# DeltaNet and SwiGLU on one core: chunk 1's second half of feed-forward units by block products, the first keys loaded in halves, 32x32 first scores, split last stores

## The chip, the core and the metric

The kernel runs on one core of a Trainium2 chip. The core has five engines that run side by side, each with its own queue in order: TensorE (PE; its weight loads are shown apart as PEld), VectorE (DVE), ScalarE (ACT), GpSimd (POOL) and SyncE (SP, which here only issues DMAs). Matmul results land in one of eight PSUM banks and have to be copied out by DVE or ACT. The metric is the device time of one execution in microseconds (us).

## The reference

Four batches, eight heads, 768 positions, head size 48. The first part is a recurrence over the positions of each head, with normalised keys; its output, 3072 tokens of 384 numbers, goes through an RMS norm and a SwiGLU feed-forward (FFN) with 1536 hidden units.

```python
k_n = k / (np.linalg.norm(k, axis=-1, keepdims=True) + 1e-06)
for t in range(S):
    y[:, :, t] = np.einsum('bhd,bhde->bhe', q[:, :, t], state)
    v_old = np.einsum('bhde,bhd->bhe', state, kt)
    state = state + bt[:, :, :, None] * np.einsum('bhd,bhe->bhde', kt, vt - v_old)
x = y, with the heads side by side                       # 3072 x 384
xn = x / np.sqrt(np.mean(x * x, axis=-1, keepdims=True) + 1e-06) * rms_g
g, val = xn @ w_gate, xn @ w_val                         # 3072 x 1536 each
out = (g * (1 / (1 + np.exp(-g))) * val) @ w_out         # 3072 x 384
```

All arithmetic is in 32-bit floats. The three weight matrices of the FFN come as 64-bit floats and are converted on the core.

## The kernel before

**Chunks.** The sequence is cut into 12 chunks of 64 positions; a chunk holds 256 tokens of the FFN. For each chunk, `prep` multiplies its keys with each other (`scores`, L690) and inverts the triangular matrix that follows from them in 15 steps of two VectorE instructions (L987, L993), `recur` applies the running state and brings the normalised tokens into the tile `xf` (chunk 1: `xp1`), and the FFN turns them into output rows. Chunk 0 has its own path, `prep_first`: it transposes the keys (`turn`), takes 64x64 scores, copies the 32x32 blocks on their diagonal into `sq1` (L775, L777), turns them into `sq2` and `at16`, multiplies those by an outer product of key norms and betas (L797, L800), and inverts 16x16 blocks in 7 steps. The key norms come from `norms`: a square on ScalarE (L711), a sum on VectorE (L712), a power on GpSimd (L715).

**The FFN has two forms.** `ffn_plain` multiplies directly: for each of 12 slices f of 128 hidden units, six matmuls of 128x128 by 128x256 (L1430, gate and value), a SiLU and a product, then two matmuls of 128x128 by 128x384 (L1412). A half is six slices; its partial output waits in `part` (`finish`). `ffn` and `down` use schemes with fewer block products: each half h of the hidden units takes 15 products of four 128x128 by 128x128 matmuls (L1523), whose results ScalarE copies and VectorE adds up in `tmp` (L1536, L1534), and the output projection takes 7 products of six 128x128 by 128x192 matmuls (L1581). For that the tokens are first combined (L1382), sums and differences of weight blocks are made by `factors(h)` (L1488; nine go to the tile `extra`, in `more`, and the last four, `over=True`, change `w_in` in place, after the last plain reader of that half) and by `out_factors` (L1560; the last changes `wo_sb` in place). Every product of half h waits for the last in-place factor (key `wx`). Before the change, chunks 0 and 1 go the plain way and chunks 2 to 11 the other. Each matmul on 32-bit floats is two instructions on PE.

**Weights.** `weights` brings them in 18 pieces through three buffers (`raw`, in `more`), each converted by two ScalarE instructions (L617, L618) and two VectorE instructions (L619, L620). The buffer `cva` lies in the part of `xf` that holds the combined tokens.

**Order.** All instructions are written into a plan with estimated durations, due times and a list of data that they read and write. `Plan.run` simulates the engines, orders each queue by due time and slack, tries random variations (those in `MOVES` are applied, each drawn from its own number) and emits the program in that order. `DUE0` and the like are due times, `FETCH`/`AHEAD` model how PE's instructions are fetched, and `EARLYM`/`MARGIN` are what is allowed beyond a DMA's estimated landing. Until `WARM`, gaps on PE are filled with matmuls on the identity matrix (`filler`, L1701) that compute nothing. So any change of an edit, a due time or `MOVES` rearranges all queues. The main sequence around the change is:

```python
if c == 1:
    stage(ffn_plain, 0, 0, FT // 2, due(0, 0))
    stage(ffn_plain, 1, 0, FT // 2, due(1, 0))
    stage(ffn_plain, 0, FT // 2, FT, due(1, 0) + 23)
    stage(ffn_plain, 1, FT // 2, FT, due(1, 0) + 46)
    stage(factors, 0)
    stage(factors, 1)
    stage(out_factors)
elif c > 1:
    stage(ffn, c, due(c, 0))
```

Of the kernel before, what the change touches and what calls it, by code (L numbers as in the profile page):

```python
# [14 lines left out]
ALU = mybir.AluOpType  # L15
# [9 lines left out]
ROUNDS, SEED = 24, 5  # L25
MOVES = (
# [7 lines left out]
)  # L34
FETCH, AHEAD = 67.0, 160.0
EARLY = 130.0
FETCH0, AHEAD0 = 42.0, 130.0
STICK = 2.0
SHAKE = 0.06
PATIENT = 0.3  # L40
RING, LANES, FIRST, LAND = 2330, 8, 1.08, 0.9
WARM = 60.0
CLEAR = (0.3, 0.6, 0.9)
TURNK = range(4, 12)
BEGIN = 1.7
ONSET = {"PE": 1.0, "ACT": 2.6, "DVE": 0.85, "POOL": 0.35, "SP": 0.5}
# [12 lines left out]
RUSH = 25.0  # L59
RUSHW = 0.0  # L60
# [38 lines left out]
class Plan:  # L99
# [197 lines left out]
    def vary(self, n, keys, past, clear, starts):  # L297
# [3 lines left out]
        a = rng.choice((rng.uniform(0.0, 650.0), rng.uniform(0.0, 220.0)))  # L301
# [77 lines left out]
def kernel(  # L379
# [248 lines left out]
    def load(c, what):  # L628
# [8 lines left out]
        for key, t, src, pr in (("k2", k2[c % NK], k, pk), ("q2", q2, q, pq)):  # L637
            for g in range(2):
                if key[0] not in what or key == "q2" and c > 1:
                    continue  # L640
                dst = t[64 * g : 64 * g + 64, :, 0:D]
                s = src.rearrange("b (y g) t e -> g t (b y) e", g=2)[g, t0 : t0 + C]
                dma(dst, s, pr, w=[(key, c % NK, g)] if key == "k2" else q2k[8 * g : 8 * g + 8], dur=0.7, work=1.5 if c < 3 else 1.15, desc=1024, eng="ACT" if c == 0 and g and key == "k2" else "SP", bulk=c > 0 or key == "q2")
# [8 lines left out]
    def turn(src, dst, keys, r, pr, split):  # L652

        for hv in range(2):
# [10 lines left out]
            P.add("PE", 0.55, tr, pr, r=r + ["ident"], w=[ps, keys[hv]], ps=ps, size=8)  # L665
# [37 lines left out]
    def kkeys_(c):  # L703
        return [("k2", c % NK, 0), ("k2", c % NK, 1)]

    def norms(c):
# [4 lines left out]
        P.add("ACT", A(768), lambda: nc.scalar.square(r_, kd), pn, r=kkeys_(c), w=[("r", 0), ("r", 1)])  # L711
        P.add("DVE", V(768), lambda: nc.vector.tensor_reduce(out=ksum[i2], in_=r_, axis=AXL.X, op=ALU.add), pn, r=[("r", 0), ("r", 1)], w=[("ksum", i2)], lat=0.05)  # L712

        P.add("DVE", 0.17, lambda: nc.vector.tensor_scalar_max(ksum[i2], ksum[i2], 1e-30), pn, w=[("ksum", i2)])  # L714
# [50 lines left out]
    def prep_first():  # L765
        kn, ktk, kkeys = k2[0], ktkeys(0), kkeys_(0)
        turn(kn, kt[0], ktk, kkeys + [("k2p", 0)], 0.0, True)
        ps = scores(kt[0], kt[0], 0.0, ktk, [])
        for q_ in range(4):
            rows, cols = slice(W * q_, W * q_ + W), slice(W * (q_ % 2), W * (q_ % 2) + W)  # L770
            for d in range(2):
                dst = sq1[rows].rearrange("p (x n) -> p x n", n=W)[:, d:16:2]
                src = lambda d=d, rows=rows, cols=cols, ps=ps: heads(ps[d])[rows, :, cols]
                if d:
                    P.add("DVE", 0.45, lambda dst=dst, f=src: nc.vector.tensor_copy(out=dst, in_=f()), 0.0, r=[ps[d]], w=[("sq1", q_, d)], last=ps[d])  # L775
                else:
                    P.add("ACT", A(256), lambda dst=dst, f=src: nc.scalar.copy(dst, f()), 0.0, r=[ps[d]], w=[("sq1", q_, d)], last=ps[d])  # L777
        sqk = [("sq1", q_, d) for q_ in range(4) for d in range(2)]
# [114 lines left out]
    def prep(c):  # L893
# [14 lines left out]
        fast = c < 4  # L908
# [199 lines left out]
    def recur(c):  # L1108
# [201 lines left out]
        for h in halves:  # L1310
# [42 lines left out]
            for p in h:  # L1353
# [7 lines left out]
                for k_ in range(KT):  # L1361
                    if c < 2 and p:
                        P.add("DVE", V(128), lambda p=p, psx=psx, k_=k_: nc.vector.tensor_scalar(
                            out=xdst[:, 2 * k_ + p], in0=psx.t[:, 128 * k_ : 128 * k_ + 128], scalar1=g_sb[:, k_ : k_ + 1], scalar2=None, op0=ALU.mult
                        ), pxv, r=[psx, "g"], w=[xkeys[p]], last=psx)
                        continue
# [3 lines left out]
        if c > 1:  # L1370
            X = lambda a, n, step=1: xf[:, a : a + step * (n - 1) + 1 : step]
            for dst, a, b_, op, n in (
                (X(6, 2), X(0, 2, 2), 4, ALU.add, 2),
                (X(8, 1), X(6, 1), 2, ALU.add, 1),
                (X(9, 2), X(1, 2, 2), 8, ALU.subtract, 2),
                (X(11, 2), X(1, 2, 2), 4, ALU.add, 2),
                (X(13, 2), X(1, 2, 2), 5, ALU.add, 2),
# [41 lines left out]
    def ffn_plain(c, f0, f1, start):  # L1419
# [317 lines left out]
```

## Time and profile before

| | |
|---|---|
| Time, median of 3 runs | 679.27 us (673.34 to 679.56) |
| The profiled execution: its own time | 678.64 us |
| its span, first to last instruction | 676.3 us |
| granted TensorE clock, mean | 0.997 |
| busy: PE / PEld / DVE / ACT / POOL | 97% / 90% / 79% / 46% / 18% |
| L1523, products of the hidden units, 2400 matmul instructions | 304.0 us busy |
| L1581, products of the output projection, 840 | 151.1 us busy |
| L1430 and L1412, plain FFN of chunks 0 and 1, 288 and 96 | 101.4 us busy |

The busy time of matmuls that follow each other closely overlaps: one L1523 instruction shows 277 ns, yet the next starts about 112 ns after it. The cost of matmul work is therefore read from the chain of work or the timeline, where a run of n instructions has a start and an end. PE's 97% also holds the filler of the first 57 us. "Idle before" is an engine's idle time ahead of an instruction, with what ended it.

### The profile page before, as it was taken

What the parts mean: (1) busy time and instruction counts of PE and PEld (TensorE: products, weight loads), DVE (VectorE), ACT (ScalarE), POOL (GpSimd) and SP (SyncE); (2) the same over time, 40 slices, a digit from 0 to 9 for tenths busy, and PEclk for the clock granted to TensorE, in tenths of its full rate; (3) what the DMA queues carried; (4) which work ended last, traced back from release to release, by engine and by line L of the source; (5) the groups of instructions that cost most, each with busy time, mean ns of one, the idle gap of its engine ahead of it and who ended that gap; (6) DMA issues with size and microseconds to landing.
All of it is one profiled execution on the core that took longest, in us unless ns stands there. A gap on an engine that the chain in (4) does not pass through costs nothing.

```text
span 676.3 us, 23308 instructions
## 1 busy us (share of the span) xinstructions
PE 658.9 (97%) x9896; PEld 608.1 (90%) x9896; DVE 535.4 (79%) x1142; ACT 314.3 (46%) x763; POOL 118.8 (18%) x95
## 2 busy tenths in 40 slices
PE   8889989999998999999999999999999999999997
PEld 5778767878798999999999999999999999999997
DVE  7988795999798598699699599599689649966472
ACT  5557572753255246346346345445353444344341
POOL 8400020020600320330330330330311012000000
PEclk9999999999999999999999999999999999999999
DMA  8984897956676246547446467525725532130101
GB/s 95 155 257 80 191 205 143 270 90 128 92 121 125 43 75 121 104 66 135 82 74 116 84 103 119 97 44 106 122 46 91 102 75 48 25 57 2 25 1 23
DMA packets 285976, 66.61 MB, mean 98 GB/s; under 512 B 269104, under 2 KB 276784, under 8 KB 285872
## 3 DMA queue, kind: packets, MB, share of 16 engines
q1 hardware_dynamic: 284832, 64.93, 53.0%
q8 instruction: 77, 1.26, 0.8%
q10 hardware_dynamic: 1040, 0.20, 0.2%
q14 instruction: 27, 0.22, 0.1%
HBM read 46.61 MB, written 18.48 MB: 96 GB/s over the span
## 4 chain that ended last, share of the span: by engine, by line
PE 79%; DVE 8%; DMA 6%; SPq 4%; issue 1%; ACT 1%; POOL 0%; DVEq 0%
PE bank L1523 37%; PE bank L1581 21%; PE bank L1430 5%; SPq L509 4%; PE bank L690 3%; PE bank L1412 2%; DVE acc L993 2%; DMA at<-dkk 2%; PE bank L1206 2%; DVE acc L987 2%; DMA q<-in_q_dram 2%; PE bank L1092 1%; PE bank L1143 1%; PE bank L1192 1%; PE bank L1131 1%
## 5 line engine op out<-in xcount | busy, mean ns | idle before, releaser
L1523 PE MATMUL bank<-xf,w_in 128*128 128x128 f32 x1440 | 179.8, 277 | 0.0
L1523 PEld LDWEIGHTS bank<-xf,w_in 128*128 128x128 f32 x1440 | 170.0, 192 | 1.6 <-issue 0.8
L1534 DVE TENSOR_TENSOR tmp<-tmp,bank 128x512 f32<-128x512 f32 x180 | 120.7, 681 | 43.6 <-PE bank L1523 37.7
L1523 PE MATMUL bank<-xf,more 128*128 128x128 f32 x960 | 124.2, 277 | 0.0
L1523 PEld LDWEIGHTS bank<-xf,more 128*128 128x128 f32 x960 | 115.1, 192 | 1.3
L1536 ACT COPY tmp<-bank 128x512 f32<-128x512 f32 x120 | 69.6, 585 | 81.9 <-PE bank L1523 67.3
L1540 ACT ACTIVATE tmp<-tmp 128x256 f32<-128x256 f32 x120 | 49.7, 417 | 82.7 <-DVE tmp L1534 82.4
L993 DVE TENSOR_REDUCE acc<-acc 128x30 f32<-128x90 f32 (+4 forms) x165 | 78.0, 473 | 5.7
L1581 PE MATMUL bank<-wo_sb,hf 128*128 128x192 f32 x360 | 65.6, 333 | 0.6 <-DVE hf L1541 0.6
L938 POOL TENSOR_TENSOR at<-at,bs 128x1024 f32<-128x1024 f32 x8 | 18.9, 2360 | 246.9 <-DMA at<-dkk 148.1
L1581 PEld LDWEIGHTS bank<-wo_sb,hf 128*128 128x128 f32 x360 | 59.1, 193 | 2.1 <-DVE hf L1541 0.9
L987 DVE TENSOR_TENSOR acc<-acc,at 128x60 f32<-128x60 f32 (+4 forms) x165 | 56.4, 342 | 2.6
L1541 DVE TENSOR_TENSOR hf<-tmp 128x256 f32<-128x256 f32 x120 | 49.6, 429 | 10.4 <-ACT tmp L1540 9.2
L715 POOL TENSOR_TENSOR knrm<-ksum,half 128x16 f32<-128x16 f32 x12 | 35.7, 2971 | 88.3 <-DVE ksum L714 45.4
L1430 PE MATMUL bank<-xf,w_in 128*128 128x256 f32 x144 | 34.4, 385 | 0.3 <-DVE w_in L620 0.3
L1412 PE MATMUL bank<-wo_sb,hf 128*128 128x384 f32 x96 | 33.9, 493 | 0.0
L1430 PE MATMUL bank<-xp,w_in 128*128 128x256 f32 x144 | 33.1, 382 | 0.0
L1327 POOL TENSOR_TENSOR rs<-ms,mhalf 128x2 f32<-128x2 f32 (+1 forms) x13 | 9.7, 748 | 126.0 <-DVE ms L1322 85.6
L1430 PEld LDWEIGHTS bank<-xf,w_in 128*128 128x128 f32 x144 | 26.6, 190 | 5.6 <-DVE w_in L620 0.9
L1430 PEld LDWEIGHTS bank<-xp,w_in 128*128 128x128 f32 x144 | 27.0, 190 | 4.7 <-issue 0.2
L1590 DVE TENSOR_TENSOR tmp<-tmp,bank 128x192 f32<-128x192 f32 x30 | 10.5, 350 | 25.7 <-PE bank L1581 25.6
L1412 PEld LDWEIGHTS bank<-wo_sb,hf 128*128 128x128 f32 x96 | 17.8, 190 | 10.4 <-DVE hf L1438 0.6
(185 smaller groups left out, 1000.8 us busy)
## 6 DMA issues: line engine op xcount, KB each, us to landing
at<-dkk SPq DMA_DIRECT2D x22, 256.0 KB, 4.2
vt<-in_v_dram SPq DMA_DIRECT2D x24, 192.0 KB, 4.2
more<-in_moe_w_gate_dram SPq DMA_DIRECT2D x6, 768.0 KB, 8.8
more<-in_moe_w_val_dram SPq DMA_DIRECT2D x6, 768.0 KB, 7.3
more<-in_moe_w_out_dram SPq DMA_DIRECT2D x6, 768.0 KB, 7.3
out_dram<-tmp SPq DMA_DIRECT2D x48, 96.0 KB, 2.2
k<-in_k_dram SPq DMA_DIRECT2D x23, 192.0 KB, 4.8
xd<-yn SPq DMA_DIRECT2D x36, 96.0 KB, 2.9
```

The lines of the kernel that those rows point to most:

```text
L509: op = P.add(eng, dur, lambda: queue.dma_start(out=dst, in_=src), prio, r, w, lat=0.1)
L715: P.add("POOL", 2.95 if c < 2 else 3.3, lambda: nc.gpsimd.tensor_tensor(out=knrm[i2], in0=ksum[i2], in1=half, op=ALU.pow), pn, r=[("ksum", ...
L987: nc.vector.tensor_tensor(out=acc[:, 1:3, 0:n, j + 2 : W].rearrange("p a i t -> p i a t"), in0=acc[:, old, 0:n, j : j + 2, None].to_broadc ...
L993: nc.vector.tensor_reduce(out=acc[:, new, 0:n, j + 2 : W], in_=acc[:, lo : lo + 3, 0:n, j + 2 : W].rearrange("p a i t -> p i t a"), axis=A ...
L1412: nc.tensor.matmul(po[p].t[:, 0:DM], hf[:, spot(f), 128 * p : 128 * p + 128], wo_sb[:, spot(f)], start=(f == f0), stop=(f == f1 - 1), skip ...
L1430: nc.tensor.matmul(ps.t[:, TOK * side : TOK * side + TOK], w_in[:, side, h_, 3 * t + i_, n : n + 128], x_[:, 2 * t : 2 * t + 2].rearrange( ...
L1523: nc.tensor.matmul(g.t[:, 128 * z : 128 * z + 128], fac[:, side, 128 * f : 128 * f + 128], xf[:, xs], start=(begin and z == 0), stop=False ...
L1534: P.add("DVE", V(512), lambda t=t, g=g: nc.vector.tensor_tensor(out=t, in0=t, in1=g.t, op=ALU.add), -1, r=[g], w=[tk], last=g)
L1536: P.add("ACT", A(512), lambda t=t, g=g: nc.scalar.copy(t, g.t), -1, r=[g], w=[tk], last=g)
L1540: P.add("ACT", A(256), lambda t=t: nc.scalar.activation(out=t[:, 0:256], in_=t[:, 0:256], func=ACTF.Silu), -1, w=[tk])
L1541: P.add("DVE", V(256), lambda t=t, f0=f0, p=p: nc.vector.tensor_tensor(out=hf[:, spot(f0) : spot(f0) + 2, 128 * p : 128 * p + 128], in0=t[ ...
L1581: nc.tensor.matmul(g.t[:, 0:192], a_[:, f], b_[:, f], start=(begin and f == 0), stop=(f == 5), skip_group_check=True)
```

## The change

Of the parts below, each is visible in the diff.

- **Chunk 1.** `ffn_plain` for chunk 1 is called for the first six slices only and without its output projection (`fold=False`). The tokens of `xp1` are combined (`combine`, moved out of `recur`), and `ffn(1)` does half h = 1 by 15 products; `down(1)` does the whole output projection of chunk 1. The order of stages is now factors(1), out_factors, factors(0).
- **First slices.** For f = 0 and 1 in `ffn_plain`, the matmuls are split into two groups of 128 tokens, each waiting only for its own tokens.
- **Chunk 0's keys** are loaded in four DMAs instead of two (two on SP's queue, two on ACT's); `turn` and `norms` of chunk 0 work on halves.
- **First scores.** `prep_first` computes 32x32 blocks of scores instead of 64x64 ones, so that two copies of 128x256 take the place of eight of 32x256.
- **Last stores.** In the last chunk each half row is stored as soon as it is added, on SP's and ACT's queues.
- **Smaller moves.** Chunk 3's scaling and first inversion step go from DVE to POOL (`FASTC`), and the second token half of chunks 0 and 1 is scaled on ACT instead of DVE (L1363). Seed, moves, due times and margins of the planner are new.

```diff
-ROUNDS, SEED = 24, 5
+ROUNDS, SEED = 24, 37
...
-FETCH, AHEAD = 67.0, 160.0
+FETCH, AHEAD = 67.0, 120.0
...
+FASTC = 3
-WARM = 60.0
+WARM = 58.0
...
-EARLYM = 0.4
-MARGIN = 1.4
+EARLYM = 0.6
+MARGIN = 1.0
-DUE0 = 44.0
-DUE1 = 70.0
-DUE2 = 156.0
+DUE0 = 38.0
+DUE1 = 82.0
+DUE2 = 154.0
-W1 = 26.0
-CV2 = 75.0
+W1 = 8.0
+CV2 = 65.0
...
+                if key == "k2" and c == 0:
+                    for hv in range(2):
+                        dst = t[64 * g : 64 * g + 64, 8 * hv : 8 * hv + 8, 0:D]
+                        s = src.rearrange("b (y g) t e -> g t (b y) e", g=2)[g, t0 : t0 + C, 8 * hv : 8 * hv + 8]
+                        dma(dst, s, pr + 0.1 * hv, w=[("k2", 0, g) if hv else ("k2h", g)], dur=0.7, work=0.75, desc=512, eng="ACT" if g else "SP")
+                    continue
...
+        for hv in range(2 if c == 0 else 1):
+            x_ = slice(8 * hv, 8 * hv + 8) if c == 0 else slice(0, 16)
...
+            P.add("ACT", A(n), lambda x_=x_: nc.scalar.square(r_[:, x_], kd[:, x_]), pn, r=kk_, w=rk)
+            P.add("DVE", V(n), lambda x_=x_: nc.vector.tensor_reduce(out=ksum[i2][:, x_], in_=r_[:, x_], axis=AXL.X, op=ALU.add), pn, r=rk, w=[ks], lat=0.05)
...
+        def squares():
+            for u in range(8):
+                for th in range(2):
+                    for d in range(2):
+                        for g in range(2):
+                            side = kt[0][64 * d : 64 * d + D, g, u, W * th : W * th + W]
+                            r0, n = 64 * g + W * th, W * u
+                            nc.tensor.matmul(pq[d].t[r0 : r0 + W, n : n + W], side, side)
...
-        fast = c < 4
+        fast = c < FASTC
...
-                    if c < 2 and p:
...
-                        continue
...
+    def combine(x_, xr, xw, pr):
...
-    def ffn_plain(c, f0, f1, start):
+    def ffn_plain(c, f0, f1, start, fold=True):
...
+            parts = ((0, 1),) if f > 1 else ((0,), (1,))
+            for tokens, (side, key) in itertools.product(parts, enumerate(("wg", "wv"))):
...
-            if f >= f0 + LAG:
+            if f >= f0 + LAG and fold:
                 down(f - LAG)
...
-        pr = (FAC, FAC + 20.0)[h]
+        pr = (FAC + 25.0, FAC)[h]
...
     def ffn(c, start):
+        if c == 1:
+            combine(xp1, [("x1", 0)], [("x1", 1)], due(1, 0) + 30.0)
+        x_, xk = (xp1, [("x1", 0), ("x1", 1)]) if c == 1 else (xf, [("xp", 0), ("xp", 1)])
-        for h in range(2):
+        for h in range(2) if c > 1 else (1,):
...
-        stage(down, c, start + 27.5)
+        stage(down, c, start + (27.5 if c > 1 else 14.0))
...
+            if c == NCH - 1:
+                for bb in range(2):
+                    tok = (2 * bb + p) * S + c * C
+                    dma(out[tok : tok + C, 192 * n : 192 * n + 192], dst[64 * bb : 64 * bb + 64], -1, r=[("oh", p, n)], w=[("out", c, p, bb, n)], desc=64, eng="ACT" if bb else "SP")
...
-            stage(ffn_plain, 1, 0, FT // 2, due(1, 0))
-            stage(ffn_plain, 0, FT // 2, FT, due(1, 0) + 23)
-            stage(ffn_plain, 1, FT // 2, FT, due(1, 0) + 46)
-            stage(factors, 0)
+            stage(ffn_plain, 1, 0, FT // 2, due(1, 0), False)
+            stage(ffn_plain, 0, FT // 2, FT, due(1, 0) + 16)
             stage(factors, 1)
             stage(out_factors)
+            stage(factors, 0)
+            P.late = True
+            stage(ffn, 1, due(1, 0) + 39)
```

More of the change, by code (lines that the diff above doesn't have):

```diff
@@ L663, in tr @@
                     )
-            P.add("PE", 0.55, tr, pr, r=r + ["ident"], w=[ps, keys[hv]], ps=ps, size=8)
+            P.add("PE", 0.55, tr, pr, r=(r if isinstance(r, list) else r[hv]) + ["ident"], w=[ps, keys[hv]], ps=ps, size=8)
             if dst is qt:
@@ L766, in prep_first @@
         kn, ktk, kkeys = k2[0], ktkeys(0), kkeys_(0)
[L767 to L778, printed above, removed]
+        turn(kn, kt[0], ktk, ([("k2h", 0), ("k2h", 1), ("k2p", 0)], [("k2", 0, 0), ("k2", 0, 1), ("k2p", 0)]), 0.0, True)
+        pq = [Group(), Group()]
+        def squares():
[6 more added lines that the diff above has]
+                            nc.tensor.matmul(pq[d].t[r0 : r0 + W, n : n + W], side, side)
+        P.rows = 32
+        P.add("PE", 1.7, squares, 0.0, r=ktk, w=pq, ps=pq, size=256)
+        P.rows = 128
+        for d in range(2):
+            dst = sq1.rearrange("p (x n) -> p x n", n=W)[:, d:16:2]
+            src = lambda d=d: pq[d].t[:, 0:256].rearrange("p (u n) -> p u n", n=W)
+            if d:
+                P.add("DVE", V(256), lambda dst=dst, f=src: nc.vector.tensor_copy(out=dst, in_=f()), 0.0, r=[pq[d]], w=[("sq1", d)], last=pq[d])
+            else:
+                P.add("ACT", A(256), lambda dst=dst, f=src: nc.scalar.copy(dst, f()), 0.0, r=[pq[d]], w=[("sq1", d)], last=pq[d])
+        sqk = [("sq1", d) for d in range(2)]
         P.add("DVE", 1.07, lambda: nc.vector.transpose(out=sq2, in_=sq1.rearrange("p (x h c) -> p c h x", h=2, c=16)), 0.0, r=sqk, w=["sq2"], port=1.0)
@@ L1490, in two @@
             if over:
[L1491 removed]
+                P.add("DVE", V(512), fn, (FAC + 35.0, FAC + 8.0)[h], r=[("ex", h)], w=[("wuse", h), ("wx", h)], port=1.0)
             else:
@@ L1529, in ffn @@
                 plain = ["begun"] if m < 3 else []
-                P.add("PE", 0.9, mm, start + 0.95 * n, r=["xc", ("xp", 0), ("xp", 1), ("wx", h)] + plain, w=[g] + first, ps=g, size=16)
+                P.add("PE", 0.9, mm, start + 0.95 * n, r=["xc", ("wx", h)] + xk + plain, w=[g] + first, ps=g, size=16)
                 n += 1
```

84 lines of the change are left out of this document (43 added, 41 removed), and 15 rows, old and new, of the table MOVES.

## The prediction

> **What bounds the kernel now.** I read the page's busy shares first, then the chain in order of time, then the timeline of the first 60 us, where the chain stops being PE. On the page PE is busy all along, and PE's products head the chain:
>
> ```profile
> PE 658.9 (97%) x9896; PEld 608.1 (90%) x9896; DVE 535.4 (79%) x1142; ACT 314.3 (46%) x763; POOL 118.8 (18%) x95
> ...
> PE bank L1523 37%; PE bank L1581 21%; PE bank L1430 5%; SPq L509 4%; PE bank L690 3%; PE bank L1412 2%; DVE acc L993 2%; DMA at<-dkk 2%; PE bank L1206 2%; DVE acc L987 2%; DMA q<-in_q_dram 2%; PE bank L1092 1%; PE bank L1143 1%; PE bank L1192 1%; PE bank L1131 1%
> ```
>
> The chain (start, us, what) gives the true rate of each kind of matmul, and the tail:
>
> ```profile
> 148.58 6.47 PE bank L1430 x30
> ...
> 175.37 7.74 PE bank L1412 x24
> 183.11 0.89 PE bank L1523 x8
> ...
> 632.47 25.01 PE bank L1523 x224
> ...
> 660.33 11.72 PE bank L1581 x72
> ```
>
> So one instruction of L1430 takes 0.2157 us, of L1412 0.3225, of L1523 0.1117, of L1581 0.1628. From 136 us on, the chain is nearly all PE. Before it, DVE, DMAs and SP are on the chain, yet PE is seldom idle there: its waits between 56 and 183 us are 2.1 us for ACT at L1358, 1.2 for DVE at L1206, 0.5 and 0.3. I read this as: **the time is the moment at which PE gets its first FFN matmul, plus all PE work after it, plus PE's stalls, plus a short tail.** The timeline shows that moment (start, us, instruction):
>
> ```profile
> 50.48 0.91 ACT L1367 ACTIVATE xf<-bank,g_sb 128x128 f32<-128x128 f32 x3
> ...
> 53.07 2.23 PE L1701 MATMUL bank<-ident 128*128 128x512 f32 x10
> ...
> 54.80 0.95 DVE L620 CUSTOM_DVE_ANT_0 w_in<-more 128x1536 uint16<-128x1536 uint16 x1
> ...
> 55.79 0.87 DVE L1363 TENSOR_SCALAR xf<-bank,g_sb 128x128 f32<-128x128 f32 x3
> ...
> 56.34 2.75 PE L1430 MATMUL bank<-xf,w_in 128*128 128x256 f32 x12
> ```
>
> The first 128 tokens are ready at 51.4, the second 128 at 56.6; PE fills 3.7 us between with L1701, which computes nothing.
>
> **The sum**, made against the profiled execution's own 678.64 us (span 676.3 and 2.3 around it; 0.6 under the median of 679.27).
>
> *PE work, -3.6.* Chunk 1's second half: 72 L1430 instructions (15.53 us) become 15 products of 8 L1523 (13.40), -2.13. Its output projection: 48 L1412 (15.48) become 84 L1581 (13.68), -1.80. The split first slices: in two slices of two chunks, 12 instructions of 0.2157 become 24 of half the width, for which I take L1523's 0.1117, +0.37.
>
> *Start of the FFN, -4.2.* (a) With split slices PE can begin on the first 128 tokens. Two slices of them are 24 instructions, 2.7 us, that now replace filler, if the second weight piece is converted before 51 (it was landed by 37.8, converted at 55.75). Bounds 0 and the whole filler, 3.7; I take 2.7. (b) The way to the first tokens gets shorter. Before, the scores ended at 9.25 and the eight copies at 12.06, since another chunk's sum (L712, 0.95) stood between them on DVE:
>
> ```profile
> 9.34 1.29 DVE L775 COPY wo_sb<-bank 32x256 f32<-32x256 f32 x3
> ...
> 10.66 0.95 DVE L712 TENSOR_REDUCE ksum<-r 128x16 f32<-128x768 f32 x1
> ...
> 11.64 0.42 DVE L775 COPY wo_sb<-bank 32x256 f32<-32x256 f32 x1
> ```
>
> After, 64 matmuls of 32x32 are 128 instructions, by L1044 (64 in 1.04) 2.1 us against 1.1, but then one copy on each engine (0.42): -2.0. Beside it runs the norm chain (rn at 14.66): halving the last square and sum saves about 0.4 each, -0.8. The product that joins both (L800, done 16.74) moves by -1 to -2, I take 1.5, with bounds 0 and 3.0 (the keys also turn earlier by half a load, 0.7). Two more key DMAs cost 0.75 of issue each on SP and ACT; behind SP's stand the eight beta loads, last landed 12.56 and used at 14.48, so this is hidden until the norm chain gains more than 1.2. The second tokens' scaling moves to ACT: 0.9 us there in a stretch where ACT is 94% busy, hidden only while the split slices give PE work.
>
> *The stall at 217 us, -1.75.* Here PE loses time to nothing that the profile names, and then runs at half clock. First the timeline, then windows of 2 us (busy time of PE, PEld, DVE, ACT, POOL, then the granted clock, the DMA share and GB/s):
>
> ```profile
> 219.31 0.49 PE L690 MATMUL bank<-qt,kt 48*64 48x64 f32 x8 [1.79 <-issue]
> ```
>
> ```profile
> 218.00:220.00 2.00, 0.69 (x20) 0.57 (x24) 1.93 (x7) 0.00 (x0) 0.00 (x0) 0.84 0.38 60
> 220.00:222.00 2.00, 2.00 (x36) 1.83 (x29) 1.19 (x5) 0.39 (x1) 0.87 (x1) 0.50 0.42 66
> 222.00:224.00 2.00, 2.00 (x12) 2.00 (x11) 0.02 (x1) 0.00 (x0) 1.92 (x2) 0.81 0.28 30
> ```
>
> The clock is 0.84, 0.50 and 0.81 in these windows, together 3.4 us at half rate, 1.7 lost on top of 1.8. A new order will not repeat it exactly, but may meet another: bounds 0 and -3.5, I take the middle. The waits of 2.1 us at 84 us did not lower the clock (1.00 from 80 to 90).
> [...]
>
> *Tail, -0.5.* The last add starts at 672.07 and takes 0.35; SP then issues two stores, 0.47 and 0.59, and the span ends 3.9 us after the add. Two queues save one issue. Bounds 0 and -1.0 (half the bytes as well).
>
> *What DVE gets and what PE must wait for, +2.0.* Chunk 1 adds nine L1534 (6.1 us), combined tokens (2.4), sums before the projection (4.1) and three adds (1.05), and loses L1404 (1.04); FASTC takes 3.4 off DVE (POOL pays 5.9, of its 18%), L1363 2.1, the first copies 1.3. Net +6 us. DVE is idle for 20.8 us between 50 and 190, but only for 1.2 between 120 and 170, where the factors lie. And PE's stock of plain work, which covered them, shrinks from 93 us to 62. Before, PE reached chunk 0's last up matmul at 149.7, and 33.3 us later, at 183, the first product. After, 7.7 us of chunk 1's projection and 4.2 of start are gone before that point: about 138. Behind it stand some 10 us of cover (two down slices, 2.6; recurrence, 7.5), in which the four in-place factors (4 x 0.69), which wait for that last up, must pass DVE's queue; every product of chunk 1 waits for the fourth. Queued behind a waiting factor are recurrence 2 and the inversions of chunk 3. Weights must come earlier too: the last conversion of `w_in` ended at 136.4, PE waited 0.3 for it, and now nine more factors (6.2 us) follow before 148. There is room, as SP issued no weight DMA from 44.5 to 68.4 and from 93.3 to 114.5. Bounds: nothing, and 19 (below). Nearest row: PE's waits of 0.3 to 2.1 for ACT and DVE between 56 and 183; I take 2.0.
>
> Sum: 678.64 - 3.56 - 4.2 - 1.75 - 0.5 + 2.0 = **670.6 us**, 1.3% under the median. About 1% is what a measurement of this kernel can tell from no change (its three runs spread by 6 us), that is 672.5 and 686.1.
>
> **Rivals.**
> *The start does not move.* DVE is an in-order queue; the first tokens waited there 2.7 us for a mean (squares done 45.1, L1322 at 47.81) behind chunk 1's inversion, and the second weight piece came at 55.75. If the new order leaves either late, parts (a) and (b) give nothing and the stall stays a matter of luck: 678.64 - 3.56 - 0.5 = 674.6. For it: DVE is 85 to 95% busy over the first 60 us. Against: the split slices need only one conversion moved.
> *VectorE becomes the bound after chunk 0 (slower).* From 147 us until chunk 2's first product, PE has 13.4 + 13.7 + 7.5 = 34.6 us of work. DVE in that stretch: evacuation of chunk 1 (6.1 + 2.6), combination 2.4, sums and adds 5.2, output factors 5.4, factors(0) 9.0, recurrence 2 6.2, inversion of chunk 3 12.2 (15 steps of 0.34 + 0.47), its norms and transposes 5.2: 54 us. If it all goes first, PE waits 54 - 34.6 = 19 us in place of my 2.0: 670.6 + 17 = 687.7. Once DVE's work ahead of that product passes 45 us the gain is gone, and at 52 the kernel is 1% slower. For it: DVE is 98% busy from 120 to 170. Against: chunk 3's 17 us are wanted only about 50 us later, and in later chunks DVE is about 80% busy.
> *All goes well.* Filler gone, 3.0 on the way, no stall, no wait: 678.64 - 3.56 - 6.7 - 3.5 - 1.0 = 663.9.
>
> **How the numbers follow.** The forecast 0.50, all well 0.08, no earlier start 0.28, DVE bound 0.14. Faster by over 1% is the first two, 0.58; within 1% the third, 0.28; slower the fourth, 0.14. The range goes from 663.9 less half the runs' downward spread (3 us), 661, to 674.6 plus a wait of 6.4 at the products, 681; past it lies most of the fourth case.
>
> **What would show it** (lines by their old numbers). First L1430 near 52, in groups of 128 columns, and less L1701 after 45. L1430 264 instructions (96 of them 128 columns wide), L1412 48, L1523 2520, L1581 924. A gap on PE between chunk 0's last L1430 and chunk 1's first L1523 of under 3 us; over 10 means that DVE has taken the end. The first 128x16 block product (L800) near 15. The prediction is wrong if PE's rate of products falls because DVE empties banks late, or if weight conversions end no earlier than 136.

## The result, and the profile after

The changed kernel takes 684.11 us (median of 20 runs, 675.67 to 687.63), the kernel before 675.96 us on the same chips (median of 20, 673.18 to 679.56). The ratio is 1.0102, 95% interval 1.0082 to 1.0123: slower by 1%, where 670.6 was forecast and 681 was the end of the range. The profiled execution of the change took 682.86 us (span 681.1, clock 0.997). Before's profiled execution, 678.64, lies 2.7 above its own median, so the two profiles stand only 4.2 apart: what follows accounts for about half of the 8 us between the medians, and the other half lies in executions that were not profiled.

Lines have moved: L1523 is now L1554 (block products), L1581 L1612 (output projection), L1430 L1454 and L1412 L1434 (plain up and down), L690 L698 (scores), L735 L748, L1367 L1386 (tokens), L1534 L1565, L941 L965 and L938 L962. From the page after, engines and groups (busy time, mean ns of one, idle time before):

```profile
PE 660.0 (97%) x10102; PEld 617.5 (91%) x10102; DVE 544.5 (80%) x1153; ACT 316.2 (46%) x775; POOL 125.8 (18%) x100
...
L1554 PE MATMUL bank<-xf,more 128*128 128x128 f32 x992 | 128.7, 278 | 5.8 <-DVE pt L748 4.0
...
L1454 PE MATMUL bank<-xf,w_in 128*128 128x256 f32 (+1 forms) x168 | 34.1, 355 | 0.2 <-ACT xf L1386 0.2
L1417 DVE TENSOR_TENSOR xf<-xf 128x256 f32<-128x256 f32 (+1 forms) x70 | 30.8, 480 | 1.9 <-ACT xf L1375 0.9
```

The products wait 5.8 us, 4.0 of them at one place. PE's busy time is no measure here, as closely following matmuls overlap in it (one of L1554 shows 278 ns, the next starts 112 ns after it). So a table beside the profile: for every two matmuls that follow each other, the distance of their starts less the steady distance for the first one's shape (112 ns for 128 columns, 216 for 256, 163 for 192, 323 for 384, 62 for L1116, 16.5 for the other small ones). What is left over is PE time that does no work: waits, switches and half clock. The work itself is 619.5 us before and 617.0 after.

```
lost PE us in     66-150  150-240  240-420  420-450  450-end   sum
before               6.3      4.6      3.2      0.8      3.3  18.2
after                5.3      6.4      5.6      6.4      2.5  26.2
```

The sum closes: from 66 us on, PE has 2.2 us less to do (587.8 and 585.6) and loses 8.0 more, and the stretch behind the last matmul is 1.0 shorter (4.3 and 3.3): +4.8, as the spans say (676.3 and 681.1). At 66 us the two kernels have done the same work to 0.3 us: the new start has gained nothing. Two losses stand out: +5.1 between 150 and 210 (0.6 and 5.7), where chunk 1's products now run, and +5.6 between 420 and 450.

**The start.** Timeline after, in order of start (us, then the idle time before and its releaser; SPq is a transfer's issue):

```profile
26.45 2.01 SPq L511 DMA_DIRECT2D vt<-in_v_dram  x1
...
32.73 1.04 PE L667 MATMUL bank<-ident,k 128*128 128x128 f32 x8
...
34.15 2.00 PE L1264 MATMUL bank<-vt,w_in 64*64 64x48 f32 x61
...
55.47 0.89 ACT L1386 ACTIVATE xf<-bank,g_sb 128x128 f32<-128x128 f32 x3
...
57.16 2.84 PE L1454 MATMUL bank<-xf,w_in 128*128 128x128 f32 x24
59.84 0.49 PE L1382 MATMUL bank<-ident,yn 128*128 128x128 f32 x3
60.26 1.16 PE L698 MATMUL bank<-qt,kt 48*64 48x64 f32 x64
61.63 0.63 PE L1454 MATMUL bank<-xf,w_in 128*128 128x128 f32 x3 [0.20 <-ACT xf L1386]
```

The split slices do what they were meant to, 24 of them run ahead of the second tokens; but the first tokens come at 55.47 and not at 50.48. That is about as late as chunk 0's first recurrence matmul, L1264, which stands at 34.15 (before: 28.62). It multiplies chunk 0's values, and in the new order the second half of these is requested at 26.45 and lands at 33.52. Before requested it at 19.53; the trace of e6, which has before's order but for one pause, shows it landed at 24.38. The runs e1 and e2 say the same: landed at 33.74 and 33.94, first matmul at 35.53 and 36.19. Meanwhile PE turns chunk 2's keys (L667, 32.73 to 33.8), and it computes chunk 2's scores (L698, 35.9 to 38.6) in the middle of that recurrence; before, these two came at 43.9 and 52.0. So the first step is late through a late load. That this is the whole delay is not shown: in the order of e9 the values are there by 25.78 and L1264 starts at 29.49, and the first tokens still come at 54.45.

The first block product, foretold for 15, ended at 18.34 (before 16.74): L824 took 1.57 us in place of 0.36, beside a multiplication on GpSimd (L762, 16.6 to 18.1). In before the product behind it (L813) took 1.55 beside the same multiplication, so that a few steps on the two are only 0.3 us apart (L853 at 20.48, before L829 at 20.15).

**427 us.** Timeline of DVE, POOL and PE after, and windows of 2 us (busy time of PE, PEld, DVE, ACT, POOL, granted clock, DMA share, GB/s):

```profile
427.00 7.17 DVE L1417 TENSOR_TENSOR xf<-xf 128x256 f32<-128x256 f32 x7
...
427.34 2.35 POOL L962 TENSOR_TENSOR at<-at,bs 128x1024 f32<-128x1024 f32 x1 [25.13 <-DMA at<-dkk]
429.77 1.74 POOL L989 TENSOR_TENSOR acc<-at 128x512 f32<-128x512 f32 x1
431.46 0.81 POOL L999 TENSOR_TENSOR acc<-acc,at 64x16 f32<-64x16 f32 x2
432.34 1.35 POOL L994 TENSOR_TENSOR at<-at,acc 128x512 f32<-128x512 f32 x1
...
435.69 1.75 PE L1554 MATMUL bank<-xf,more 128*128 128x128 f32 x8 [4.01 <-DVE pt L748]
```

```profile
432.00:434.00 2.00, 0.00 (x0) 0.00 (x0) 2.00 (x4) 0.87 (x2) 1.61 (x2) 1.00 0.00 0
...
436.00:438.00 2.00, 2.00 (x12) 2.00 (x11) 0.24 (x1) 0.00 (x0) 0.00 (x0) 0.52 0.00 0
438.00:440.00 2.00, 2.00 (x56) 1.77 (x57) 0.00 (x0) 0.59 (x1) 0.00 (x0) 0.63 0.00 0
```

The seven additions that combine a chunk's tokens take 2.4 us elsewhere and 7.17 here, where GpSimd's four multiplications and one addition for another chunk run at the same time. Three of the seven take 2.39, 1.92 and 1.50 us in place of 0.42, ending 0.15, 0.28 and 0.28 us after a GpSimd instruction. What stands behind them on DVE (L748) is late, PE idles for 4.01 us and then runs at about half clock for 3.4 us.

### The profile page after: what moved, and what is told of

It is laid out like the page before. It is cut to its first block, busy times and chain, and to the rows that moved or that the text cites. A ratio compares the mean times of both kernels' runs of the same rounds, so it can differ in the third digit from the quotient of the medians.

```text
span 681.1 us, 23759 instructions
## 1 busy us (share of the span) xinstructions
PE 660.0 (97%) x10102; PEld 617.5 (91%) x10102; DVE 544.5 (80%) x1153; ACT 316.2 (46%) x775; POOL 125.8 (18%) x100
## 5 line engine op out<-in xcount | busy, mean ns | idle before, releaser
L1554 PE MATMUL bank<-xf,w_in 128*128 128x128 f32 x1496 | 185.9, 277 | 0.1
L1554 PEld LDWEIGHTS bank<-xf,w_in 128*128 128x128 f32 x1496 | 176.5, 193 | 1.3 <-ACT tmp L1567 0.2
L1565 DVE TENSOR_TENSOR tmp<-tmp,bank 128x512 f32<-128x512 f32 x189 | 126.6, 679 | 36.0 <-PE bank L1554 32.4
L1554 PE MATMUL bank<-xf,more 128*128 128x128 f32 x992 | 128.7, 278 | 5.8 <-DVE pt L748 4.0
L1554 PEld LDWEIGHTS bank<-xf,more 128*128 128x128 f32 x992 | 119.5, 192 | 8.0 <-DVE pt L748 4.3
L1612 PE MATMUL bank<-wo_sb,hf 128*128 128x192 f32 x396 | 71.0, 329 | 0.0
L962 POOL TENSOR_TENSOR at<-at,bs 128x1024 f32<-128x1024 f32 x9 | 21.4, 2377 | 259.6 <-DVE bs L965 117.9
L1612 PEld LDWEIGHTS bank<-wo_sb,hf 128*128 128x128 f32 x396 | 63.8, 190 | 1.0 <-DVE hf L1572 0.2
L1454 PE MATMUL bank<-xf,w_in 128*128 128x256 f32 (+1 forms) x168 | 34.1, 355 | 0.2 <-ACT xf L1386 0.2
L1417 DVE TENSOR_TENSOR xf<-xf 128x256 f32<-128x256 f32 (+1 forms) x70 | 30.8, 480 | 1.9 <-ACT xf L1375 0.9
L1617 ACT COPY tmp<-bank 128x192 f32<-128x192 f32 x33 | 10.5, 317 | 45.6 <-PE bank L1612 43.4
L1454 PEld LDWEIGHTS bank<-xf,w_in 128*128 128x128 f32 x168 | 27.8, 190 | 3.9 <-ACT xf L1386 0.3
L1737 PE MATMUL bank<-ident 128*128 128x128 f32 (+2 forms) x88 | 24.3, 415 | 1.4 <-POOL ident masks.py:199 1.4
L1303 DVE COPY u<-bank 128x384 f32<-128x384 f32 x11 | 6.1, 554 | 24.1 <-PE bank L1216 17.7
```

What stands on the lines that cost most here:

```text
L1417: P.add("DVE", V(128 * n), lambda dst=dst, a=a, b_=b_, op=op: nc.vector.tensor_tensor(out=dst, in0=a, in1=b_, op=op), pr, r=xr, w=["xc", ( ...
L1454: nc.tensor.matmul(ps.t[:, TOK * side + n0 : TOK * side + n1], w_in[:, side, h_, 3 * t + i_, n : n + 128], x_[:, 2 * t : 2 * t + 2].rearra ...
L1554: nc.tensor.matmul(g.t[:, 128 * z : 128 * z + 128], fac[:, side, 128 * f : 128 * f + 128], (x_ if xs < 6 else xf)[:, xs], start=(begin and ...
L1565: P.add("DVE", V(512), lambda t=t, g=g: nc.vector.tensor_tensor(out=t, in0=t, in1=g.t, op=ALU.add), -1, r=[g], w=[tk], last=g)
L1612: nc.tensor.matmul(g.t[:, 0:192], a_[:, f], b_[:, f], start=(begin and f == 0), stop=(f == 5), skip_group_check=True)
L1737: nc.tensor.matmul(warm[:, 0 : 128 * w_].rearrange("p (w n) -> p w n", n=128), ident, ident[:, None, :].to_broadcast([128, w_, 128]))
```

## The experiments

Theories at the outset: A, the new order breaks where engines run apart from the planner's reckoning; B, VectorE has too much to do around chunk 1's scheme; C and D, the start is late through the halved keys or through early weight conversions. Each ratio is to the kernel before on the same chip.

**e1_gate**, the collision taken out. In the finished order, for chunks 3 to 10, and nothing else:

```diff
+        for copy, scale in self.gates[2:]:
+            one = next(x for x in turns if x[0] is copy)
+            turns.remove(one)
+            turns.insert(next(i for i, x in enumerate(turns) if x[0] is scale), one)
```

> The changed kernel in its own order; only VectorE's small copy `bs` (old place: well ahead) is put directly ahead of GpSimd's scaling of `at` in the order of chunks 3 to 10, so that GpSimd can't start its four multiplications before VectorE has come that far (VectorE has then done the token combination). Theory A (the new order breaks where engines run apart from the plan): the combination at 427 us takes 2.4 us again and not 7.2, PE's idle stretch of 4.0 us at 432 and the half clock behind it (1.7) go, and the time falls by 5 to 7 us, to about 677.5, a ratio of 1.002 to the kernel before. Theory B (VectorE simply has too much to do): the combination is faster, but PE waits for VectorE at another place soon after; the ratio stays at 1.008 or above.

Measured 679.4 us, ratio 1.0043 (1.0021 to 1.0065), against 1.0102: 4 to 5 us of the 8. Timeline of the run at the same place:

```profile
431.70 2.41 DVE L1417 TENSOR_TENSOR xf<-xf 128x256 f32<-128x256 f32 x7
...
435.50 0.17 DVE L965 COPY bs<-beta_b 128x32 f32<-128x32 f32 x1
...
435.80 2.36 POOL L962 TENSOR_TENSOR at<-at,bs 128x1024 f32<-128x1024 f32 x1 [28.80 <-DMA vt<-in_v_dram]
```

The additions take 2.41 again, PE loses 0.8 between 420 and 450 (was 6.4). The collision is shown as the cause of that loss in this order. The kernel stays slower than before.

**e2_keys_whole** (`dst = t[64 * g : 64 * g + 64, :, 0:D]`, the second half's transfer left out), **e3_no_early_weights** and **e4_no_factors0** take one suspect away each (e3 and e4 leave work out, so their outputs differ; the first pair of lines is e3's, for one of the four instructions, the second e4's):

```diff
-  nc.scalar.activation(out=top, ...)
+  None if n < 5 else nc.scalar.activation(out=top, ...)
...
-  fn()                                    # factors(0), not in place
+  nc.scalar.copy(out_, w_(0, 0))          # six of nine, three left out
```

> The changed kernel in its own order; the first chunk's keys come by two DMAs as before the change, not by four. Theory C (the start lost time through the halved keys): all keys are there at about 6.2 us and not 7.9, the first block product ends 1 us earlier or more (17.3, was 18.3), the first tokens at 54.5 instead of 55.5, and the time falls by 0.5 to 1. Theory D (the start is held by the weight conversions): the block product may move, the first tokens stay within 0.3 us, and the time doesn't change.

> The changed kernel in its own order, with the conversions of the first five weight pieces left out (two ScalarE and two VectorE instructions each; GpSimd writes a constant into those weights instead, so the FFN of all chunks computes with other weights). Theory D (these conversions, put ahead of the first tokens, hold the start): the first tokens come at about 50.5 instead of 55.5 and the first up matmul at 52; the time falls by 3 to 5 us. Theory A: the start moves by as much, but the later stalls take most of it, and the time falls by less than 2. Theory C: the first tokens move by less than 1 us.

> The changed kernel in its own order, with the nine additions that make half 0's combined weights left out on VectorE (6.2 us, at 114 and 154 to 167 us; ScalarE copies six blocks of the plain weights there instead, so chunks 2 to 11 compute with other weights). Theory B (VectorE's load around chunk 1's scheme costs PE time): PE's waits of 3 us between 152 and 165 us go, and the time falls by 2 to 4. Theory A: the waits there go, but the end moves by less than 1.5, since the stall at 432 stays.

e2: 683.22, ratio 1.0107 (1.0070 to 1.0144). The first block product starts at 17.28, with halves at 16.7 to 17.1: the halves help by 0.2 to 0.6 us, and the first tokens (56.63) lie within the 55.5 to 57.2 of the runs of this order with halves. C falls. e3: 682.62, ratio 1.0099 (1.0072 to 1.0126); the first tokens come at 54.86, 0.6 under the earliest of the other runs of this order, where D expected 5. D falls as the main cause; L1264 stands at 34.05 there, as late as in the change. e4: 684.47, ratio 1.0134 (1.0097 to 1.0170). Waits of PE between 150 and 210 us (waited for: us in total, times, longest), first after, then e4:

```profile
PE bank L1554 <- DVE tmp L1565: 1.8, 2, 1.1
PE bank L698 <- DVE tmp L1565: 0.9, 1, 0.9
PE bank L1092 <- DVE tmp L1565: 0.3, 1, 0.3
```

```profile
PE bank L1554 <- DVE tmp L1565: 1.3, 2, 0.7
PE bank L1554 <- ACT tmp L1567: 0.5, 2, 0.3
```

With 6.2 us less on DVE the named waits fall from 3.0 to 1.8 and PE's loss there only from 5.7 to 5.6; nothing reaches the end. So the amount of DVE's work in these factors does not decide the end, as B had it. The test is not quite clean, since the copies that stand in for them bring ScalarE into the list (0.5).

**e5_gate_spread and e6_before_spread** go after the pauses named issue. Ops are put later in the finished order:

```diff
+        best = best[0], later(turns, ((1507, 1512), (931, 617)))    # e5
+        best = best[0], later(best[1], ((989, 840), (948, 842)))    # e6, in the kernel before
```

> The changed kernel with the copy `bs` moved as in the run e1_gate, and two groups of 64 small score matmuls each put behind two block products on TensorE: the one at 334 us, before which the traces of this change show 235 to 245 TensorE instructions (loads and matmuls) in 2 us, a pause of 1.1 to 1.7 us named issue, a transfer issue of SyncE that takes 1.2 to 2.1 us in place of 0.45 at the same time, and half clock for 3.4 us; and the one at 166 us, which waited 1.3 us for a transfer. Theory E (TensorE runs out of fetched instructions when too many short ones stand in a row while SyncE's queue is full): the pause and the half clock at 334 go (-3.2), the wait at 166 too (-1.3); against e1_gate the time falls by 3 to 4.5, to about 675.5, level with the kernel before. Theory F (the pause comes from the transfers alone): it stays or moves with them, and the time falls by 1.3 at most.

> The kernel before, its own order; at 216 to 221 us, where its trace shows a pause of 1.79 us named issue after 243 TensorE instructions in 2 us and 3.4 us at half clock behind it, one slice of the down projection is put between the group of small recurrence matmuls and the group of 64 score matmuls, and one more ahead of the next small group. Theory E: pause and half clock go and the time falls by 3 (1.8 + 1.7, less the half that a new order costs), a ratio of 0.995. Theory F: within 0.2% of the kernel before.

e6: 674.4, ratio 0.9976 (0.9951 to 1.0000). Timeline and a window of e6, where before had stood still for 1.79 us:

```profile
216.00 2.22 PE L1581 MATMUL bank<-wo_sb,hf 128*128 128x192 f32 x12
218.15 1.16 PE L690 MATMUL bank<-qt,kt 48*64 48x64 f32 x64
219.24 2.22 PE L1581 MATMUL bank<-wsum,tmp 128*128 128x192 f32 x12
```

```profile
220.00:222.00 2.00, 2.00 (x41) 1.65 (x40) 2.00 (x6) 0.00 (x0) 1.48 (x1) 1.00 0.38 60
```

The 64 score matmuls now run through, the clock stays at 1.00, PE's loss in 210 to 240 falls from 4.0 to 1.4; 1.6 us of the 3 expected appear in the time, just at the edge of what is measurable. e5: 679.92, ratio 1.0061 (1.0039 to 1.0083), no gain over e1 (1.0043). Its longest gap near 334 is 0.85 (1.52 in e1) and PE's loss from 316 to 345 falls from 3.9 to 2.6, but near 166 one wait of 1.33 becomes two, of 0.87 and, at 169, of 0.58, and 345 to 420 loses 0.5 more. Theory E's cure works on both pauses; it earns 1 to 2 us in before's order and nothing in the new one, where 3 to 4.5 were expected.

**e8_slices_twice** tests what the start is worth, by making it dearer:

```diff
-  def mm(side=side, ps=ps, n0=n0, n1=n1):
+  def mm(side=side, ps=ps, n0=n0 if len(tokens) > 1 or c else 0, n1=n1):
```

> The changed kernel in its own order; the four slices of chunk 0's first two up units over the second tokens compute the first tokens again as well (24 matmul instructions of 256 columns in place of 128), 2.7 us more of TensorE work between 61 and 67 us, the same output. If TensorE's work from its first up matmul on sets the end, as the prediction's terms for the start take for granted, the time grows by 2.4 to 2.7, a ratio of 1.014. If VectorE's work sets the end between 60 and 180 us (the prediction's slower rival), the added time is hidden and the time grows by less than 1.

Measured 683.13, ratio 1.0085 (1.0051 to 1.0119): 2.7 us more of PE work, and no more time. The timeline of e8 shows the added work. The two lists of waits between 66 and 150 us (first after, then e8) show what becomes of the waits behind it:

```profile
62.89 2.86 PE L1454 MATMUL bank<-xf,w_in 128*128 128x256 f32 x12 [0.20 <-ACT xf L1386]
```

```profile
PE bank L1068 <- DVE r L1192: 0.8, 1, 0.8
...
PE bank L1434 <- DVE hf L1465: 0.5, 1, 0.5
PE bank L1230 <- DVE u L1303: 0.5, 1, 0.5
```

```profile
PE bank L1382 <- ACT yn L1357: 0.6, 2, 0.3
PE bank L1230 <- DVE u L1303: 0.6, 1, 0.6
```

PE's loss from 66 to 120 us falls from 4.2 to 2.1: the added work fills waits, for DVE above all (L1192, L1465), that come anyway. By the same reading an earlier first up matmul would have waited there longer, in this order; that was not run.

**The order itself.** e7 runs the change in the planner's first order; e9 and e10 its edits with two planner values as before and a new search for MOVES; e11 to e13 the kernel without any edit in three other orders; e14 the change with another list.

```diff
-MOVES = (30000001, ...)
+MOVES = ()                                     # e7; e12 in the kernel before
...
-PATIENT, MARGIN = 0.0, 1.0
+PATIENT, MARGIN = 0.3, 1.4                     # e9, e10
...
-AHEAD, STICK, PATIENT, MARGIN = 160.0, 2.0, 0.3, 1.4
+AHEAD, STICK, PATIENT, MARGIN = 120.0, 0.5, 0.0, 1.0    # e11, in the kernel before
+MOVES = (61000000, ...)                        # new lists: e9 to e11, e13, e14
...                                             # e11 takes SHAKE, CLEAR, ONSET and EARLYM over too
```

> The changed kernel with the list MOVES empty, so with the planner's first order: by its own reckoning it ends at 675.8, with the list at 666.1. Theory A (the gain in the reckoning is not kept when the kernel runs): the time is at most 4 above that of the change, 680 to 688. Theory G (the reckoning is right about the difference, and what is lost is lost in every order alike): about 10 above it, 692 to 696.

> All edits of the change, but MARGIN 1.4 and PATIENT 0.3 as in the kernel before, and a list MOVES found anew with about the same effort; by the planner's reckoning it ends at 669.6 (the change 666.1, the kernel before 670.1). Theory A (the edits are worth what TensorE saves, the change's own order lost it): PE loses less than 2 us at every place after 240 us, and the time is 2 to 4 under the kernel before, a ratio of 0.995. Theory H (the edits cost more than they save, in any order): PE's loss between 150 and 210 us stays at 5 to 6 against 0.6 before, and the ratio is 1.004 or above.

> The kernel of e9_replan_edits with the copy `bs` moved as in e1_gate. Theory A: as e9_replan_edits, or 1 to 5 less if a combination there collides with GpSimd; a ratio of 0.990 to 0.996, under both kernels. Theory H: 1.000 or above.

> None of the edits; the kernel before with the change's planner values (AHEAD 120, STICK 0.5, PATIENT 0, MARGIN 1.0 and the others of these) and a list MOVES found anew with about the same effort; by the reckoning it ends at 669.4 (the kernel before 670.1). If these values make orders that the chip doesn't keep (theory A), the ratio is 1.005 to 1.012 with no edit at all. If the edits are what costs (theory H), the ratio is within 0.998 to 1.003.

> The kernel before with the list MOVES empty; by its own reckoning it ends at 672.9, with its list at 670.1. Theory A2 (the time of a kernel is that of its order, and the order of the kernel before happens to be one that the chip keeps; other orders of the same work lose 8 to 10 us more to short stalls): 682 to 687, a ratio of 1.009 to 1.016. Theory I (orders are alike but for what the reckoning says, and the edits or the planner's values cost): 677 to 679.

> The kernel before, its edits and its planner values untouched, with another list MOVES found in the same way with about as many tries; by the reckoning it ends at 664.9, 5.2 sooner than its own order. Theory A2: 680 to 687 in spite of that, so a ratio of 1.006 to 1.016 from the order alone. Theory I: 669 to 672.

> The changed kernel, its edits and its planner values untouched, with another list MOVES found in the same way; by the reckoning it ends at 666.9 (its own list 666.1). Theory A2: 679 to 687, near the other orders of the edits (683 to 684); the mean of the edits' orders lies 2 to 3 under that of the orders without them, which is what TensorE saves. Theory I: 684, as the change itself.

"Reckoned" is the end of the plan by the planner; "lost" is PE's sum from 66 us on in the profiled execution.

| run | edits | order | reckoned | measured | ratio (95%) | lost |
|---|---|---|---|---|---|---|
| before | no | its own | 670.1 | 675.96 | 1 | 18.2 |
| e6 | no | its own, one pause removed | | 674.4 | 0.9976 (0.9951 to 1.0000) | 14.6 |
| e11 | no | the change's values, new list | 669.4 | 685.68 | 1.0148 (1.0118 to 1.0178) | 25.0 |
| e12 | no | own values, no list | 672.9 | 685.74 | 1.0143 (1.0105 to 1.0181) | 26.6 |
| e13 | no | own values, new list | 664.9 | 682.9 | 1.0104 (1.0069 to 1.0139) | 22.0 |
| after | yes | its own | 666.1 | 684.11 | 1.0102 (1.0082 to 1.0123) | 26.2 |
| e1 | yes | its own, collision removed | | 679.4 | 1.0043 (1.0021 to 1.0065) | 24.1 |
| e7 | yes | own values, no list | 675.8 | 683.19 | 1.0112 (1.0081 to 1.0143) | 22.4 |
| e9 | yes | two values as before, new list | 669.6 | 682.92 | 1.0119 (1.0081 to 1.0156) | 25.2 |
| e14 | yes | own values, new list | 666.9 | 682.49 | 1.0090 (1.0060 to 1.0121) | 23.1 |

e10 (683.25, ratio 1.0104, 1.0072 to 1.0135) is e9 with the gate and gains nothing. A combination does collide in e9, at 378 us (two additions of 2.53 and 1.98 us in place of 0.42), and none in e10; but behind it PE waits only 0.7 us for DVE in e9, where it was 4.0 in the change. What a collision costs depends on what waits behind it. In e14 no combination collides, and the order is slow all the same.

Every newly planned order, with the edits or without, takes 682.5 to 685.7 us. e13 is the plainest: not one edit, the same planner values, an order that ought to end 5.2 us sooner, and it is 1% slower. Its longest PE waits, from the table of waits, and two windows behind the second of them:

```profile
PE bank L1523 <- ACT tmp L1536: 2.9, 1, 2.9
PE bank L1358 <- ACT yn L1333: 2.6, 1, 2.6
PE bank L1131 <- issue: 1.6, 1, 1.6
```

```profile
86.00:88.00 2.00, 1.54 (x7) 1.46 (x8) 1.09 (x3) 1.86 (x8) 0.40 (x1) 0.60 0.95 117
88.00:90.00 2.00, 2.00 (x4) 1.04 (x4) 1.86 (x8) 1.84 (x4) 0.00 (x0) 0.55 0.99 354
```

The list of e11's waits begins with others:

```profile
PE bank L1523 <- DVE tmp L1534: 3.4, 2, 2.5
PE bank L1192 <- DMA mt<-dx: 3.1, 2, 2.9
PE bank L1291 <- issue: 2.0, 1, 2.0
```

Each order has its own stalls of 1.5 to 4 us, one to three of them, at other places and with other releasers. They are not the whole difference: before has two as well (2.15 at 84 us, 1.79 at 217), e7 and e14 have one each (1.7 and 1.9). The rest is many short waits. The column "lost" also leaves out the start: the PE work still to do at 66 us is 587.8 us in before, 586.7 to 590.6 in e11 to e13 and 585.7 to 589.8 with the edits. Theory A held in e7 (G, by which the reckoning is right, expected 692 to 696), but missed in e9 and e10, which it put under the kernel before. Theory H (the edits cost) foretold the ratios of e9 and e10 rightly, but not e11, which was to stay within 0.998 to 1.003 and has the highest ratio of all; I (orders are alike but for the reckoning) falls with e12 and e13. What is left is A2: the order decides, and the kernel before has an uncommonly good one. Between the groups there is little: three replanned orders without edits take 684.8 on average, four with them 683.2, a difference of 1.6 in the direction of the 2.5 that PE saves, no larger than the spread within each group.

**e15_before_spread_tail**, one part of the change alone, on e6's order:

```diff
+  for bb in range(2 if c == NCH - 1 else 0):
+      (nc.scalar if bb else nc.sync).dma_start(out=out[tok(bb) : tok(bb) + C, 192 * n : 192 * n + 192], in_=dst[64 * bb : 64 * bb + 64])
```

> The order of e6_before_spread (674.4) with one part of the change alone: the last chunk's tokens are stored by halves of the columns, each right behind its own addition, from SyncE and ScalarE. The prediction gave this part 0.5 (0 to 1.0), the profile after the change shows 0.9 between the last projection matmul and the end: 673.5 to 674.0, a ratio to the kernel before of 0.996, under both kernels. If the stores were hidden anyway: 674.4.

Measured 674.18, ratio 0.9980 (0.9962 to 0.9998), not told apart from e6. Behind the last matmul the profile shows 3.5 us in place of 4.2. It is faster than both kernels, by 0.2%, with an interval that just leaves out 1, and by some 1.2%.

## Why the prediction failed

The forecast was 670.6; 684.11 came. Of the 13.5 us between, 2.7 lie in the starting point, as before's profiled execution was that much above its median of 20. The forecast takes before's profiled execution, subtracts what each edit saves in it, and leaves the rest of the order where it stood. Step by step:

- **PE work, -3.56: right in mechanism.** The counts came out as foretold: L1454 264, L1434 48, L1554 2520, L1612 924. The ledger has -2.5: the 64 more small instructions of the first scores add 1.0, which lies in the start.
- **Start, -4.2: failed, and the first step to fail.** Both halves took it that the first tokens stay at 50.5 or come sooner, and the second that the way to them is the inversion alone. They came 5 us later: the recurrence behind the inversion also needs chunk 0's values, whose second half the new order lands at 33.5 (read from the traces; not tried by itself, and e9 shows that early values alone don't bring the tokens back). The block product came 1.6 later, not 1.5 sooner. The prediction looked for the obstacle in the conversions; e3 shows that these are worth 0.6 to 2.4 at the tokens. And e8 shows that in this order 2.7 us of PE work at that place change the end by nothing, so the price per microsecond was wrong too: "the moment at which PE gets its first FFN matmul, plus all PE work after it, plus PE's stalls" is no sum of independent terms, since a later start shortens the stalls.
- **The stall at 217 us, -1.75, bounds 0 and -3.5: the step that decides.** It did go: the loss between 210 and 240 fell from 4.0 to 0.7. But "may meet another" was bounded by no gain, as if the new order could at worst have one stall of the same size. From 66 us on the new order loses 8.0 more than the old one, 5.6 of it at 427 us. Nothing in the profile of before could show that place, but nothing there kept a new order to one stall of 3.5 either. Three orders of the unedited kernel put a price of 7 to 10 us on being replanned; the sum had it at -1.75.
- **Waits at chunk 1's products, +2.0: right in mechanism, too small against before's order.** DVE's evacuation is what PE waits for (3.0 by name); PE's loss between 150 and 210 is 5.1 above before. Before's own 0.6 there is again uncommonly good: e11, e12 and e13, without edits, lose 2.0, 4.4 and 2.8 between 150 and 210, and the four orders with them (after, e7, e9, e14) 5.7, 6.1, 4.2 and 6.8, which is 2.6 more on average. Chunk 0's last up matmul ends at 140.4 (138 foretold) and the first product starts 5.0 later, but PE is at work in between (16 down matmuls, L1434), so nothing of the slower rival's 19 is there. Of the queue that the prediction names, e4 took out half 0's nine factors: 5.6 of 5.7 stay. The four in-place factors and half 1's nine were not taken out, so what makes the evacuation late is open.
- **Tail, -0.5: right;** 1.0 in the profile, too small for the measured times.
- **Half clock behind a stall.** The bound of -3.5 holds 1.7 us of half clock behind the pause of 1.8, from before's row. Pauses of much the same length differ in this: the one of 1.79 us at 217 and one of 2.08 at 178 in e12 were followed by half clock (windows at 0.50), pauses of 1.64 (e13, 219 us) and 1.97 (e11, 89 us) were not (1.00). The last section says what tells them apart in the traces.

Of the rivals, "the start does not move" named what happened there, at 674.6; "VectorE becomes the bound" had the right sign and nearly the right time (687.7) by luck: the 19 us of waiting that it rests on are 3.0 in the trace.

What stays open: why the order of the kernel before is so much better than others with the same or a better reckoning. That it was picked by its time on the chip is a guess. So is what the edits are worth in an order as good; 1 to 3 us by the work saved and by the two groups.

## What to carry to other kernels

When an order comes out of a search and the kernel is tuned to a few per cent, a change that makes the search run again has a term of its own: what the present order is worth over a fresh one. Measure it by replanning the unchanged kernel a few times before crediting any edit, and judge edits over several orders. A saving at the start counts only if no wait behind it takes it up; adding the same amount of idle work there is a quick test.

## What the runs showed of the hardware

- **Three of VectorE's additions took about as long as the GpSimd instructions beside them.** A 128x256 addition (L1417), 0.42 us alone, took 2.39 beside a GpSimd instruction of 2.35, 1.92 beside one of 1.74 and 1.50 beside one of 1.35, and ended 0.15, 0.28 and 0.28 us after it. With GpSimd's instructions moved behind them (e1), the seven together took 2.41 again, not 7.17. The surprise was the price at the end: 4.8 us more on an engine busy for 80% of the span became 5.6 of lost PE time, and 4 to 5 of the run.
- **In these traces half clock followed the idle time within fixed intervals, not the length of one pause.** The clock records of before and after each show one stretch at half clock ahead of the last matmul, 3.413 us long. In all 17 traces such stretches begin a whole number of 3.413 us after the first clock record (in before 215.04 us, 63 times; in after 430.08, 126 times). Cut into these intervals, between 66 and 665 us and at full clock, PE's lost time sorts them: all 14 intervals with 2.3 us or more lost were followed by half clock, 3 of the 10 with 2.1 to 2.3, and 2 of the 2935 with less. The pause of 1.79 us in before lies in one interval, which loses 2.5 with the small waits around it (in after, the interval ahead of the half clock loses 3.1); those of 1.97 in e11 and 1.64 in e13 are split between two, of which none loses more than 1.8.
- **Pauses named issue go with the longest bursts of small matmuls.** In the 17 traces, between 66 and 665 us, none of 235 bursts of 250 to 261 weight loads and matmuls within 2 us was followed by such a pause of over 0.5 us, and 10 of 15 bursts of 262 to 279 were, by 0.9 to 2.1 us (276 in before, then 1.79 us; 272 in after, then 1.10). The burst is no full account: five passed, two of them in e13 (270 at 172 us, 279 at 574), and six pauses of 0.7 to 2.0 us came without one (three in e11). A transfer issue on SP of 1.2 to 2.1 us in place of 0.45 stands beside each of the ten, but no better tells them apart: in before one of 2.02 at 294 us stood beside a burst of 259 that passed. What PE lacks in these pauses no trace shows; fetched instructions, as in theory E, are the author's guess.
